# Buffers, order and PSUM sharing in a fused attention and expert kernel: a second fp16 buffer for q and k, later gate transposes, copied logits, earlier gathers

## The chip, the cores and the metric

The kernel runs on one core of one Trainium2 chip. The metric is the device time in microseconds (us) of one execution. A "span" is the time from the first to the last instruction in a profile, 1.4 to 2.1 us shorter than the time of the same execution. Each run has several executions: one with a profile, and, where rounds are named, timed ones that alternate with the kernel before on the same chip.

An execution is marked slow when it is over 1.5% above the fastest of its kernel. On this one core that mark needs care. In five sets of rounds the kernel before spreads from 218.64 us (at a clock of 0.930) to 232.84 us (0.900) without a clear gap. In the first set no execution was below 225 us, and there 9 of the 11 count as fast; in the other sets only one to four do. So I give medians with the lowest and highest, and beside them the ratio of fast runs where there is one.

## The reference

Attention over B=4, H=8, S=768, D=64: three "retrieval" heads (0, 2 and 6) are causal over all keys, the other five see 4 sink keys and a window of 64. Its output, seen as 3072 rows of 512, goes through a mixture of experts that skips some rows:

```python
skip_score = x @ w_skip                      # rows with a score <= 0 stay as they are
logits = x[do_compute] @ w_gate              # 8 experts, the best one is taken
gate_w = softmax(logits)[best]
y[mask_e] = gate_w * (relu(x[mask_e] @ w1[e]) @ w2[e])     # 512 -> 1024 -> 512
out[do_compute] = x + y
```

## The kernel before

Attention works on 16 pairs of heads, four pairs to a batch. The loop tells the work of one iteration; TensorE takes its instructions in exactly this order, the order on the other engines is a scheduler's.

```python
for i in range(NPR + 2):                     # NPR = 16 pairs
    cast_v(i); load_qk(i + 3); load_v(i + 2) # cast: fp32 -> fp16 on GpSimd
    step(0)                                  # a step: score matmuls into PSUM, exp on ScalarE
    transpose(i + 1, "q")                    # TensorE -> tr_psum, copied out by ScalarE
    step(1)
    if i >= 2: gate_transpose(i - 2)         # "xtp": TensorE -> tr_psum, copied out by VectorE
    weigh(i - 1, 0)                          # weighting with v
    step(2)
    transpose(i + 1, "k")                    # TensorE -> tr_psum, "kz" copies, most on VectorE
    cast_qk(i + 2)                           # "qin", "kin" on GpSimd
    step(3)
    weigh(i - 1, 1)                          # ends with the fp16 copy "gx" on GpSimd
    step(4)
    if (i - 2) % 4 == 0 and i > 2: place((i - 2) // 4 - 1)   # counts "kps" in tr_psum
    gate_logits(i - 2)                       # every fourth time: logits "gps" in tr_psum, choose(b)
```

`tr_psum` has two buffers, for the q transposes, the k transposes, the gate transposes, the logits and the counts alike. PSUM is full. The fp32 q, k and v have two buffers each, filled by the sync engine's DMA queue; the expert weights come over GpSimd's queue.

`choose(b)` is a chain of some thirteen small VectorE operations on the logits of a batch (`mx`, `sub`, `eq`, `m2`, `oh`, `rk`, `gate`, `val`). It reads `gpss[b]`, the logits, in PSUM. `place(b)` counts tokens for each expert (matmuls into `kps`) and works out each token's place (`posi`, `Lall`, `Rall` on VectorE). After the last batch the index table `idx_s` is ready, and the expert half starts: gather 128 rows at a time, two matmul groups per expert, scatter.

```python
for e in range(E):
    if e + 1 < E:
        first(e + 1)                         # first matmul group of the next expert
        t = 2 * (e + 4)
        if t < NT: gather(t, t + 2)          # GpSimd: indirect DMA of the rows
        if todo: load_weight()               # GpSimd: 1 MB of weights
    ...
```

The softmax here doesn't subtract the row's maximum and nothing guards it: scores larger than these inputs give would overflow.

## Time and profile before

| | before |
|---|---|
| time, median of the first three runs | 228.5 us (225.91 to 229.19) |
| profiled execution | 221.96 us, span 220.5, clock 0.922 |
| attention, first score matmul to `idx_s` | 11.85 to 134.1 us |
| expert half, `idx_s` to the end | 86.4 us |

The page's first part gives for each engine the busy time, its share of the span and the number of instructions:

```profile
PE 153.5 (70%) x1829; PEld 117.2 (53%) x1829; DVE 127.8 (58%) x307; ACT 95.9 (43%) x134; POOL 131.7 (60%) x206
```

PE is TensorE, DVE VectorE, ACT ScalarE and POOL GpSimd. No engine is full.

### The profile page before, as it was taken

To read this page: it belongs to the slowest core of one execution; us is meant where nothing else is said; L and a number is where in the kernel's file an instruction comes from. 1 tells how busy PE (TensorE), PEld (TensorE's weight loads), DVE (VectorE), ACT (ScalarE), POOL (GpSimd) and SP (SyncE) were. 2 spreads that over 40 slices of the span, in tenths; PEclk is the share of its full clock that TensorE was granted. 3 is DMA by queue.
4 is the path that set the end of the run, shared out by engine and by line. 5 is a ranking of instruction groups with operands and counts; after the bars stand their busy time and mean duration, and the time that the engine had idled before them with its cause. 6 is when DMAs were issued, how large, how long until landed. Compare 5 with 4: busy or idle time off the path is not lost. (4 is left out here: it accounts for less than half of the span.)

```text
span 220.5 us, 4689 instructions
## 1 busy us (share of the span) xinstructions
PE 153.5 (70%) x1829; PEld 117.2 (53%) x1829; DVE 127.8 (58%) x307; ACT 95.9 (43%) x134; POOL 131.7 (60%) x206
## 2 busy tenths in 40 slices
PE   0277777786676569668976620489999999399900
PEld 0256556675465457556865510377866886247300
DVE  7519687669996399966899572342453453121400
ACT  2156875876766584656854210044412431204000
POOL 7999788676873686756765114883678344212510
PEclk9999999999999999988996965589999999969985
DMA  6987999999699997899999978999999999961010
GB/s 158 271 273 191 295 199 328 268 253 307 185 224 253 314 328 183 212 263 197 239 219 245 197 172 174 195 253 251 210 195 214 252 217 265 234 177 56 17 60 1
DMA packets 47982, 47.09 MB, mean 214 GB/s; under 512 B 28484, under 2 KB 43588, under 8 KB 47058
## 3 DMA queue, kind: packets, MB, share of 16 engines
q0 software_dynamic: 7104, 21.56, 46.8%
q1 hardware_dynamic: 40850, 25.17, 41.5%
q8 instruction: 16, 0.26, 0.5%
q14 instruction: 12, 0.10, 0.1%
HBM read 56.64 MB, written 10.49 MB: 304 GB/s over the span
## 5 line engine op out<-in xcount | busy, mean ns | idle before, releaser
L591 ACT ACTIVATE at<-pst 128x1024 f16<-128x1024 f32 (+2 forms) x76 | 61.6, 833 | 41.0 <-PE pst L586 40.8
L918 ACT ACTIVATE ht<-hps 128x512 f16<-128x512 f32 x32 | 19.1, 597 | 54.2 <-PE hps L911 54.2
L586 PE MATMUL pst<-qT,kz 128*128 128x128 f16 (+2 forms) x288 | 36.5, 247 | 0.2
L586 PEld LDWEIGHTS <-kz 128*128 128x128 f16 x288 | 24.4, 103 | 20.6 <-issue 5.6
L930 POOL DMA_INDIRECT out_dram<-xg,idx_s x16 | 16.3, 1019 | 29.0 <-DVE xg L928 21.5
L911 PE MATMUL hps<-xT,w 128*128 128x256 f16 x256 | 30.9, 281 | 1.2 <-DVE xT L901 1.2
L911 PEld LDWEIGHTS <-w 128*128 128x128 f16 x256 | 28.5, 115 | 3.9 <-issue 1.5
L925 PE MATMUL yps<-w,ht 128*128 128x512 f16 x128 | 30.3, 393 | 0.0
L525 DVE COPY kz<-tps 64x768 f16<-64x768 f16 x28 | 26.5, 948 | 6.3 <-PE tps L508 5.9
L928 DVE SCALAR_TENSOR_TENSOR xg<-yps,gsl,xg 128x512 f32<-128x512 f32 x16 | 12.0, 751 | 22.0 <-PE yps L925 22.0
L577 PE MATMUL pst<-smask,ident 128*128 128x512 f16 (+1 forms) x60 | 22.7, 378 | 2.3 <-ACT at L591 2.3
L652 PE MATMUL xtp<-ident,gx 128*128 128x128 f16 x96 | 8.4, 225 | 21.3 <-POOL gx L634 10.4
L875 POOL DMA_INDIRECT xg<-out_dram,idx_s x16 | 16.8, 1052 | 10.1 <-issue 4.0
L489 POOL CAST kin<-kf 128x768 f16<-128x768 f32 x16 | 14.0, 875 | 13.8 <-PE tps L508 13.3
L925 PEld LDWEIGHTS <-ht 128*128 128x128 f16 x128 | 12.7, 101 | 14.6 <-issue 1.9
L611 PE MATMUL opsa<-va,at 128*128 128x65 f16 x372 | 19.9, 196 | 0.0
L652 PEld LDWEIGHTS <-gx 128*128 128x128 f16 x96 | 5.6, 99 | 24.9 <-POOL gx L634 18.1
L626 DVE TENSOR_TENSOR xh<-opsa,rec 128x384 f32<-128x384 f32 x32 | 17.8, 556 | 1.2
L634 POOL CAST gx<-xh 128x768 f16<-128x768 f32 x15 | 12.3, 822 | 10.1 <-DVE xh L626 10.1
L611 PEld LDWEIGHTS <-at 128*128 128x128 f16 x472 | 18.3, 100 | 0.1
L891 DVE CAST x<-xg 128x512 f16<-128x512 f32 x16 | 9.4, 626 | 14.5 <-DMA xg<-out_dram,idx_s 14.5
L495 POOL CAST va<-vf 128x768 f16<-128x768 f32 x16 | 13.2, 828 | 7.1 <-PE opsa L611 5.0
(120 smaller groups left out, 257.7 us busy)
## 6 DMA issues: line engine op xcount, KB each, us to landing
w<-in_moe_w_dram POOLq DMA_DIRECT2D x14, 1024.0 KB, 11.4
qf<-in_q_dram SPq DMA_DIRECT2D x16, 384.0 KB, 5.7
kf<-in_k_dram SPq DMA_DIRECT2D x16, 384.0 KB, 5.0
vf<-in_v_dram SPq DMA_DIRECT2D x32, 192.0 KB, 5.3
out_dram<-xh SPq DMA_DIRECT2D x7, 768.0 KB, 5.3
w<-in_moe_w_dram POOLq DMA_DIRECT2D x4, 512.0 KB, 7.2
out_dram<-xh SPq DMA_DIRECT2D x2, 384.0 KB, 3.7
xg<-out_dram,idx_s POOLq DMA_INDIRECT x16, 6.9
```

The lines of the kernel that those rows point to most:

```text
L489: nc.gpsimd.tensor_copy(h16, qk32[name, i].rearrange("p h n d -> p n h d"))
L525: nc.vector.tensor_copy(to, ti[r])
L577: nc.tensor.matmul(pst[:, bank - c0:bank - c0 + mw], C.ident, neg[:, bank:bank + mw], start=True, stop=False)
L586: nc.tensor.matmul(pst[:, c - c0:c - c0 + n * P], kb, qT[i][:, qb * P:(qb + n) * P], start=mw <= 0, stop=mw <= 0 or (c, j, qb, n) == here[-1])
L591: nc.scalar.activation(ats[i][:, b0:b0 + cn], pst[:, :cn], ACT.Exp, scale=SCALE)
L611: nc.tensor.matmul(opsa[:, qb, :], ats[i][:, b0 + c:b0 + c + P], vb, start=(n == 0), stop=(n == len(plan) - 1))
L626: nc.vector.tensor_mul(xhs[i // 2][:, :, 2 * (i % 2) + hi, :], opsa[:, :, :D], rec.to_broadcast([P, NQB, D]))
L875: ins = nc.gpsimd.indirect_dma_start(out=xgs[t], out_offset=None, in_=out[:, :], in_offset=bass.IndirectOffsetOnAxis(ap=idx_s[:, t:t + 1], ...
L911: nc.tensor.matmul(hps[:, fi, :], wts[e, 0][:, s].rearrange("p (t c r) -> p t r c", c=P, r=WR)[:, fs // WR, fs % WR], xTs[e][:, s, :], sta ...
L918: nc.scalar.activation(ht[:, 2 * f2:2 * f2 + 2], hps, ACT.Relu)
L925: nc.tensor.matmul(yps, hts[e][:, fs, s2 * P:(s2 + 1) * P], wts[e, 1][:, fs, :], start=(fs == 0), stop=(fs == FS - 1))
L930: ins = nc.gpsimd.indirect_dma_start(out=out[:, :], out_offset=bass.IndirectOffsetOnAxis(ap=idx_s[:, t:t + 1], axis=0), in_=xgs[t], in_off ...
```

## The change

The intent is to take away waits in front of the gate transposes (by asking for them later, and by freeing the PSUM buffer of the logits at once), a wait of GpSimd (by second fp16 buffers), and a hole before the last expert (by gathering its rows earlier).

```diff
-         tc.tile_pool(name="qk_in", bufs=1) as qk_in_pool, \
+         tc.tile_pool(name="qk_in", bufs=2) as qk_in_pool, \
@@ choose(b)
-            lg, skip = gpss[b][:, :, :E], gpss[b][:, :, E]
+            glog = gpss[b]
+            if b < B - 1:
+                glog = small("glog", [P, NQB, E + 1])
+                nc.vector.tensor_copy(glog, gpss[b])
+            lg, skip = glog[:, :, :E], glog[:, :, E]
@@ the attention loop
                 step(1)
-                if i >= 2:
-                    gate_transpose(i - 2)
                 ...
                 step(3)
+                if i >= 2:
+                    gate_transpose(i - 2)
@@ the expert loop
-                    t = 2 * (e + 4)
-                        gather(t, t + 2)
+                    t = 4 * (e + 2)
+                        gather(t, t + 4)
```

## The prediction

> **What bounds the kernel now.** The program has two halves: attention (16 head pairs, four to a batch, gating of the finished batch woven in), and the expert part (gather, two matmuls per expert, scatter). No engine is full over the span (TensorE 70%, VectorE 58%, GpSimd 60%), so I first cut the span into stages at the places where the timeline shows the first score matmul of each group of four pairs, and asked for busy time in those stretches. Columns: stretch, its length, busy time and count on TensorE, weight loads, VectorE, ScalarE, GpSimd, then clock, DMA share, GB/s.
>
> ```profile
> 11.85:37.24 25.39, 19.65 (x265) 15.50 (x265) 16.35 (x27) 18.03 (x24) 22.25 (x36) 1.00 0.95 252
> 37.24:63.72 26.48, 20.52 (x339) 16.54 (x339) 22.33 (x57) 18.80 (x26) 19.92 (x32) 1.00 0.96 261
> 63.72:93.08 29.36, 20.52 (x339) 16.55 (x339) 23.49 (x58) 18.80 (x26) 19.18 (x31) 1.00 0.96 249
> 93.08:122.90 29.82, 22.82 (x327) 18.31 (x327) 23.61 (x59) 18.32 (x25) 18.20 (x31) 0.89 1.06 232
> ...
> 141.90:189.00 47.10, 46.32 (x352) 35.41 (x351) 18.88 (x34) 16.15 (x28) 28.21 (x31) 0.96 1.04 234
> 189.00:198.20 9.20, 5.58 (x24) 2.54 (x25) 2.70 (x5) 0.57 (x1) 0.66 (x2) 0.81 0.83 205
> ```
>
> In attention the fullest engine is VectorE, but only at 22.33/26.48 = 84%, 80% and 79% in groups 2 to 4 (64% in the first, which has no gating). So attention is bound by waits round a loop of engines, with VectorE closest behind. In the expert part TensorE is full (46.32 of 47.10 us) until 189, and then has a hole.
>
> Next, the waits of the attention stages: who waited for whom, total, times, longest.
>
> ```profile
> PE xtp L652 <- POOL gx L634: 10.4, 7, 2.3
> PE pst L577 <- ACT at L591: 5.8, 10, 0.8
> PE xtp L652 <- DVE rk L719: 4.8, 3, 1.8
> PE xtp L652 <- DVE posi L756: 4.6, 3, 1.9
> ```
> ```profile
> DVE gxT L660 <- PE xtp L652: 13.9, 8, 3.3
> ```
> ```profile
> POOL kin L489 <- PE tps L508: 13.3, 10, 2.3
> ```
>
> TensorE loses 10.4 + 4.8 + 4.6 = 19.8 us in front of one operation, the gate transpose (xtp): 10.4 because GpSimd has not yet cast the attention output to fp16 (gx), 9.4 because the shared PSUM buffer it wants is still held by the routing logits (read last by rk) or by the routing counts. VectorE then idles 13.9 us in front of the copy of that transpose, and GpSimd 13.3 us because its one fp16 k buffer is still being transposed. The chain that ended last holds only two pieces at the very end (0.5% of the span) and does not help here.
>
> The hole at 189 is in the timeline:
>
> ```profile
> 188.97 0.60 ACT L918 ACTIVATE ht<-hps 128x512 f16<-128x512 f32 x1 [0.28 <-PE hps L911]
> 191.83 1.13 DVE L891 CAST x<-xg 128x512 f16<-128x512 f32 x2 [5.60 <-DMA xg<-out_dram,idx_s]
> 192.49 0.23 PEld L898 LDWEIGHTS <-x 128*128 128x128 f16 x4 [3.83 <-DVE x L891]
> 192.50 1.13 PE L898 MATMUL xtp<-ident,x 128*128 128x128 f16 x8 [3.56 <-DVE x L891]
> ```
>
> The last expert's rows are gathered too late: GpSimd issued the second of those gathers at 179.7, after 2.6 us of its own waiting for an earlier weight load, and its rows landed some 11 us later.
>
> **What the Trainium skill says.** "Perfetto Trace Analysis", section Optimization Strategy, says that a gap repeating on the engine that should be saturated can mean too few buffers for the next tile. The trace agrees: the gap in front of xtp repeats in 13 of the iterations, 0.5 to 2.3 us each. "TensorE: Matmul & The Clock Gate", Part 1, says that the clock drops to half after about 3.4 us of idleness and needs about as long of work to come back. The trace fits: after the 3.56 us hole the clock of that stretch is 0.81, and the 16 matmuls that begin at 193.42 run 4.95 us until the next group starts, where the 16 that begin at 181.82 run 3.46. "SBUF — State Buffer", section Who interferes with whom, says that VectorE in a two-port mode and GpSimd block each other for whole instructions. The trace fits that too: one form of copy, 64x20 (kx), takes 146 ns at least and 2447 ns at most. So a VectorE packed more tightly beside GpSimd will not reach 100%.
>
> **The change, part by part.**
>
> *Gate transpose later.* On TensorE's list it moves from before the first weighting to after the k transposes, that is behind 0.3 to 0.7 us of weighting, 0.3 of k transposes and about 1.2 of scores: 1.8 to 2.2 us by the timeline around 46 to 48.7. The waits for gx are 0.5 to 2.3 us, so practically all of the 10.4 us goes. The two PSUM buffers are then taken in the order q, k, gate transpose, not q, gate transpose, k. That puts the next waiter on the logits' or counts' buffer at the k transposes, later in the iteration.
>
> *Logits copied out.* One added VectorE copy in each of three batches, about 0.2 us each by the reduction that reads the same logits (202 ns): +0.6 us of VectorE. It frees the PSUM buffer before the choice of experts, which takes about 4 us from mx to the last val. With the new order the 4.8 us go; the 4.6 us for the counts go mostly through the order alone.
>
> *Two buffers for fp16 q and k.* Removes GpSimd's 13.3 us of waiting, which helps only because the late casts stand in front of gx on the same engine and hold the load buffers. No instruction is added.
>
> *Sum for attention.* 19.8 us of TensorE waits are removed, but I don't count them all: behind them stands VectorE. Group by group I let VectorE run at 92%, my choice, between the 84% of now and the full use that the blocking by GpSimd forbids; its busiest 10 us stretches show 95%. Group 2: (22.33 + 0.2)/0.92 = 24.5 for 26.48, gain 2.0. Group 3: 23.7/0.92 = 25.8 for 29.36, gain 3.6. Group 4: 23.8/0.92 = 25.9 for 29.82, gain 3.9. Group 1 isn't VectorE bound: the one wait there, 2 us, goes. Together 11.5. Another 1 us from the tail, where the first weighting of the last pair no longer stands behind the gate transpose; and 2 us back, because weight loads and q, k, v loads are squeezed into less time (v issues already stall on their queue, up to 9.5 us at 93). Attention: minus 10.5 us.
>
> *Gathers four at a time.* Eight gathers are issued in the first two turns and not in four. An issue costs GpSimd about 1.3 us (1.04 plus 0.3), so in turns 0 and 1 the weight loads start 2.7 us later each, and in turns 2 and 3 earlier; the last weight load goes out some 7 us sooner. The last gathers are issued near 164, not 180, and needed near 188. The first matmuls of successive experts start at 155.49, 162.88, 170.28, 177.67, 185.06 and 198.16: 7.39 us apart, but 13.10 the last time. The excess, 5.7 us (3.6 wait, 1.5 slow clock, 0.6 transposes that no longer overlap), should go. I count 4.5, since the DMA engines are at 1.04 in this stage and a late weight may take the place of the late rows.
>
> Sum: 10.5 + 4.5 = 15 us of 220.5, leaving 205.5, or 6.8%.
>
> **Rivals.**
> (a) VectorE takes over at once: its gating work is lumped (the choice in one iteration of four, the counts in the next), so TensorE waits there instead, for kz or for PSUM. For it: 95% in the stretches with gating, at 50 to 60, 80 to 90 and 110 to 120. Against: two weighting buffers and two score buffers give some slack. Then attention gains only 5 us, in all 9 to 10, and the profiled span is 211.
> (b) DMA takes over. For it: share 0.95 to 1.06 throughout and stalls of the queue that loads v. Against: it moved 323 GB/s at 70 to 80 us but 215 at 80 to 90, so it has room. If attention is cut and the expert part then starves for weights, the gain of one half is lost: 212 to 214.
> (c) VectorE packs almost fully and the hole goes wholly: 11.5 + 4 + 5.7, some 21 us, 199 to 200.
> (d) The early gathers delay weights of experts 4 and 5. Against: those have 10 us and more between landing and use. It would cost at most the 4.5 us.
>
> **Range and chances.** The profiled execution (222 us in all) is quicker than the timed ones (225.9 to 229.2), so I scale: 228.5 x 205.5/220.5 = 213. As the timed executions may have a lower clock, with less to gain from waits, I say 214. The range 208 to 221 spans rival (c) to rivals (a) and (b): 228.5 x 200/220.5 = 207 and 228.5 x 213/220.5 = 221. Over 2% faster means below 223.9: only if two rivals meet. Chances 0.91 faster, 0.07 within, 0.02 slower.
>
> **What would show it.** Right: no wait of TensorE for gx over 1 us in total; the group of waits for rk and posi below 2 us; GpSimd's wait for the k transposes gone; groups 2 to 4 at 24 to 26 us with VectorE at 90% or more; successive experts 7.4 us apart to the end with no wait for a gather after 150. Wrong: a new wait of similar size at the k transposes or the weighting; VectorE still near 80% in groups 2 to 4; expert matmuls that wait for weights; the first gather, now 5 us from issue to landing, queued behind weights.

## The result, and the profile after

| | before | after |
|---|---|---|
| median | 228.45 us, 4 runs (225.91 to 229.19) | 220.86 us, 4 runs (219.36 to 222.55) |
| ratio of fast runs | | 0.9689, interval 0.9599 to 0.9779 |
| span of the profile | 220.5 us | 218.4 us |
| `idx_s` ready | 134.1 us | 137.4 us |
| from `idx_s` to the end | 86.4 us | 81.0 us |

A ratio is the mean time of one kernel's fast runs over that of the other's in the same rounds, so not quite the ratio of the medians quoted. The change is 3.1% faster. The expert half gained 5.4 us, for 4.5 foretold. The attention half of these two profiles lost 3.3 us, where 10.5 should have come.

The same stretches as in the prediction, cut at the first score matmul of each group of four pairs, then the tail up to `idx_s`, then the stretch in which the hole was. Columns: stretch, its length, busy time and count on TensorE, weight loads, VectorE, ScalarE, GpSimd, then clock, DMA share, GB/s.

```profile
11.92:36.24 24.32, 19.66 (x264) 15.61 (x264) 16.44 (x26) 17.87 (x23) 21.40 (x35) 1.00 0.88 225
36.24:66.77 30.53, 23.47 (x342) 19.34 (x340) 23.60 (x58) 18.64 (x26) 21.47 (x33) 0.89 0.91 262
66.77:92.11 25.34, 20.43 (x340) 16.88 (x339) 23.53 (x56) 18.47 (x26) 20.41 (x32) 1.00 1.03 281
92.11:125.68 33.57, 23.16 (x326) 18.66 (x326) 24.08 (x63) 18.00 (x24) 16.02 (x28) 0.85 0.89 200
125.68:137.40 11.72, 6.05 (x103) 5.32 (x101) 8.32 (x34) 1.22 (x3) 1.82 (x4) 0.65 0.89 175
...
189.00:198.00 9.00, 9.00 (x71) 6.94 (x70) 4.10 (x7) 2.77 (x5) 2.83 (x4) 1.00 1.03 217
```

Of groups 2 to 4 only the third did what was expected: 25.34 us with VectorE at 23.53/25.34 = 93%. The second group became 4 us longer than before (30.53 for 26.48), the fourth, 33.57 us, is the longest of all, and both have a clock of 0.85 to 0.89. TensorE is full from 189 to 198: the hole is gone.

The waits of the same profile (who waited for whom: total, times, longest):

```profile
POOL va L495 <- DMA vf<-in_v_dram: 9.7, 1, 9.7
PE kps L747 <- DVE kz L525: 8.2, 3, 3.5
PE xtp L652 <- POOL gx L634: 8.1, 4, 4.7
...
POOL kin L489 <- DMA kf<-in_k_dram: 4.1, 5, 1.7
...
POOL qin L489 <- DMA qf<-in_q_dram: 3.6, 1, 3.6
```

The waits of the gate transposes for `rk` and `posi` are gone, and GpSimd's 13.3 us of waiting for the k transposes too (which part of the change removed that is asked below). In their place stand three new things. The counts (`kps`) wait 8.2 us for VectorE's copies of k. GpSimd waits 9.7 us, once, for a v load, and 7.7 us for q and k loads. The gate transposes still wait 8.1 us for GpSimd's copy `gx`.

The single wait of 9.7 us in GpSimd's own timeline (start, length, engine, line, operation, and in brackets the idle time before it):

```profile
110.90 0.85 POOL L501 COPY vx<-va 4x325 f16<-4x325 f16 x2
121.42 0.83 POOL L495 CAST va<-vf 128x768 f16<-128x768 f32 x1 [9.67 <-DMA vf<-in_v_dram]
```

And the same cast, of the same pair 15, in the profile before:

```profile
114.43 0.82 POOL L495 CAST va<-vf 128x768 f16<-128x768 f32 x1 [1.70 <-PE opsa L611]
```

The second half of pair 15's v was asked for at 103.19 us and landed at 121.27, 18.1 us later; before it was asked for at 104.44 and landed 4.7 us later. I counted the DMA records of the two queues by microsecond in the trace of the changed kernel:

```
us      GpSimd's queue (weights)             sync engine's queue (v, results)
106      0 records                           461 records
108     27, median 0.32 us each              489, median 0.02 us each
110     50, median 0.32                       21, median 0.03
112     51, median 0.32                       24, median 0.03
116     23, median 0.62                       10, median 0.03
119      5                                   373, median 0.05
```

As long as large weight records run, the v load gets only one small record for every two of them. The Trainium skill, "DMA: Bandwidth & Descriptors", section Queues, rings and completion order, says that a DMA engine takes turns between the queues it has work for, packet by packet. The traces agree in part. In the second profile of the kernel before (b_again, below) the counts are about equal, 53 and 50 records in the microsecond from 112, 29 and 30 in that from 114, with 0.3 to 0.6 us a record on one side and 0.03 on the other. In the changed kernel they are two to one; no run here shows why.

### The profile page after: what moved, and what is told of

The parts are those of the page before. A ratio compares the mean times of both kernels' runs of the same rounds, so it can differ in the third digit from the quotient of the medians.

```text
span 218.4 us, 4660 instructions
## 1 busy us (share of the span) xinstructions
PE 156.9 (72%) x1829; PEld 122.1 (56%) x1829; DVE 129.4 (59%) x310; ACT 95.4 (44%) x134; POOL 132.4 (61%) x206
## 5 line engine op out<-in xcount | busy, mean ns | idle before, releaser
L591 ACT ACTIVATE at<-pst 128x1024 f16<-128x1024 f32 (+2 forms) x76 | 60.7, 836 | 44.7 <-PE pst L586 44.5
L586 PE MATMUL pst<-qT,kz 128*128 128x128 f16 (+2 forms) x288 | 38.5, 255 | 2.0 <-DVE kz L525 1.9
L586 PEld LDWEIGHTS <-kz 128*128 128x128 f16 x288 | 25.4, 106 | 25.5 <-issue 9.2
L915 PE MATMUL hps<-xT,w 128*128 128x256 f16 x256 | 31.5, 285 | 1.2 <-DVE xT L905 1.2
L934 POOL DMA_INDIRECT out_dram<-xg,idx_s x16 | 16.8, 1052 | 22.6 <-DVE xg L932 19.1
L929 PE MATMUL yps<-w,ht 128*128 128x512 f16 x128 | 28.8, 379 | 0.0
L611 PE MATMUL opsa<-va,at 128*128 128x65 f16 x372 | 21.7, 203 | 0.0
L495 POOL CAST va<-vf 128x768 f16<-128x768 f32 x16 | 13.3, 832 | 13.3 <-DMA vf<-in_v_dram 9.7
L611 PEld LDWEIGHTS <-at 128*128 128x128 f16 x472 | 20.2, 105 | 1.0 <-issue 0.5
L489 POOL CAST qin<-qf 128x768 f16<-128x768 f32 x16 | 14.3, 891 | 9.8 <-DMA qf<-in_q_dram 3.6
L929 PEld LDWEIGHTS <-ht 128*128 128x128 f16 x128 | 12.3, 98 | 13.4
L905 DVE COPY xT<-xtp 128x512 f16<-128x512 f16 x16 | 6.1, 420 | 14.8 <-PE xtp L902 14.7
L516 ACT ACTIVATE qT<-tps 128x768 f16<-128x768 f16 x16 | 12.9, 805 | 4.5 <-PE tps L508 4.5
```

Source lines behind the costliest of these rows:

```text
L489: nc.gpsimd.tensor_copy(h16, qk32[name, i].rearrange("p h n d -> p n h d"))
L586: nc.tensor.matmul(pst[:, c - c0:c - c0 + n * P], kb, qT[i][:, qb * P:(qb + n) * P], start=mw <= 0, stop=mw <= 0 or (c, j, qb, n) == here[-1])
L591: nc.scalar.activation(ats[i][:, b0:b0 + cn], pst[:, :cn], ACT.Exp, scale=SCALE)
L611: nc.tensor.matmul(opsa[:, qb, :], ats[i][:, b0 + c:b0 + c + P], vb, start=(n == 0), stop=(n == len(plan) - 1))
L915: nc.tensor.matmul(hps[:, fi, :], wts[e, 0][:, s].rearrange("p (t c r) -> p t r c", c=P, r=WR)[:, fs // WR, fs % WR], xTs[e][:, s, :], sta ...
L929: nc.tensor.matmul(yps, hts[e][:, fs, s2 * P:(s2 + 1) * P], wts[e, 1][:, fs, :], start=(fs == 0), stop=(fs == FS - 1))
```

## The experiments

All 18 runs gave correct results. The five sets of rounds ran on chips 0, 6, 15, 0 and 12, and each has its own runs of the kernel before: 227.31 us (225.25 to 228.99) in the first, 225.71 (221.06 to 227.81) in the second, 227.08 (221.33 to 230.6) in the third, 227.4 (223.75 to 229.19) in the fourth, 226.85 (218.64 to 232.84) in the fifth, 11 runs each.

| run | what | median us (lowest to highest) | ratio of fast runs | `idx_s` in its profile |
|---|---|---|---|---|
| first set | | | | |
| b_again | before, unchanged | 227.48 (226.49 to 228.29) | 1.0033 | 139.0 |
| g_only | gathers only | 223.02 (214.85 to 224.85) | none | 139.8 |
| attn_only | the attention parts only | 224.15 (222.82 to 226.13) | 0.9906 | 136.6 |
| a_again | the change, unchanged | 220.42 (217.49 to 221.59) | 0.9636 | 137.9 |
| second set | | | | |
| w_move | change, weight loads moved | 222.93 (221.74 to 224.64) | 1.0014 | 141.3 |
| v3 | change, third v buffer | 213.60 (210.66 to 215.78) | 0.9504 | 130.4 |
| p_early | change, counts earlier | 223.04 (220.5 to 224.87) | 0.9958 | 139.4 |
| tl_only | later transposes and logits copy | 221.23 (220.2 to 225.74) | 0.9936 | 132.1 |
| third set | | | | |
| tlg | change without second q, k buffers | 215.49 (214.65 to 216.56) | 0.9701 | 132.2 |
| v3_tlg | tlg with third v buffer | 213.03 (212.12 to 214.72) | 0.9600 | 131.5 |
| v3_again | v3 once more | 213.62 (210.15 to 216.48) | 0.9522 | 127.1 |
| b_v3 | before with third v buffer | 219.81 (216.2 to 220.65) | 0.9773 | 131.2 |
| fourth set | | | | |
| ch | change, choice later | 218.80 (215.91 to 224.7) | 0.9615 | 134.8 |
| v3_ch | v3, choice later | 217.70 (216.34 to 221.68) | 0.9630 | 135.8 |
| v3_tlg_ch | v3_tlg, choice later | 214.94 (214.45 to 216.15) | 0.9541 | 131.7 |
| v3_few | v3, four weight loads out of attention | 234.90 (233.29 to 236.53) | 1.0414 | 129.3 |
| fifth set | | | | |
| v3_kz | v3_tlg, four copies to ScalarE | 213.08 (212.76 to 214.24) | none | 130.9 |
| v3_kzx | v3_kz, 15 more copies to ScalarE | 206.69 (205.14 to 208.11) | none | 123.0 |

In the second and third set the fast runs of before are only its two or three quickest (221.06, 222.35 and 224.34; 221.33 and 222.78), so those ratios make the gains look smaller than the medians do. Neither is wrong; they answer to different parts of the spread. With so few fast runs the verdicts at 2% are weak: a_again is faster, b_again and attn_only are the same, g_only, v3_kz and v3_kzx have none, and all others are unclear. So I also read the stages in the profiles. A difference between runs of two sets is one between chips too.

### Was the first profile of the kernel before a typical one, and what is each half worth?

**b_again** and **a_again** have no edit. **g_only** has only the last part of the diff (gathers), **attn_only** all the others.

> The kernel before, unchanged, run and profiled once more. Its first profile (221.96 us) was 4 to 7 us quicker than its timed executions (225.91 to 229.19). Theory 'lucky profile': the first profile is not the typical execution; this one comes out at 226 to 229 and shows more waiting in the attention half (longer waits in front of the gate transpose, or for a v load), with the idea that some load sometimes lands late. Rival 'clock': the waits are the same within 1 us and the granted clock is lower, below 0.90. Ratio to itself 1.00 within 0.5%.

> Before, with only the gathers four at a time. By the two traces the hole of 5.7 us in front of the last expert should go: theory 'the gain is the gathers' expects 4.5 to 6 us less, ratio 0.974 to 0.980, first matmuls of successive experts 7.4 us apart to the end. Rival 'the weights are next': the late rows are replaced by late weights of the last expert and the ratio is above 0.99.

> The changed kernel without the new gathers: two buffers, later gate transpose, copied logits. Theory 'the gain is the gathers': the three attention parts together are worth nothing, ratio 0.99 to 1.01, with the waits of TensorE for gx cut but 5 to 10 us of new waits (routing counts behind the k copies, GpSimd casts that wait for loads). Rival 'attention does gain in the typical execution': ratio 0.975 to 0.985, because the first profile of before was a quick one.

> The changed kernel, unchanged, profiled once more. In its first profile one v load of 192 KB took 18.1 us to land (the others 2.8 to 11.7) and held GpSimd for 9.7 us and TensorE for 4.7. Theory 'built in': the same load of the last pair is late again, by 14 us or more, since weight packets of 0.3 to 0.6 us alternate with its packets of 0.02. Rival 'chance': it lands in under 8 us this time and the span is 3 to 5 us shorter than 218.4. Ratio to before 0.96 to 0.98.

The waits of the second profile of the unchanged kernel before:

```profile
PE xtp L652 <- POOL gx L634: 17.9, 8, 7.1
...
POOL va L495 <- DMA vf<-in_v_dram: 8.2, 1, 8.2
```

The late v load is in the kernel before as well. The first profile, on which the prediction rests, was an execution without it: 221.96 us against 227.48. The clock is not what differs by much (0.922 and 0.911). In this profile, of an execution of 228.29 us, the gate transposes wait not 10.4 but 17.9 us for `gx`; the copy stands behind the cast of v on GpSimd.

The gathers alone bring 227.31 - 223.02 = 4.3 us, and on top of the attention parts 224.15 - 220.42 = 3.7. Predicted were 4.5. One of the six executions of g_only took 214.85 us; it has no profile, so why is open. Beside it the other five are marked slow, so there is no ratio; but the profiles agree. From `idx_s` to the end it is 85.8 to 87.7 us in the five with the old gathers (before, b_again, attn_only, tl_only, b_v3), and 80.0 to 81.4 in seven with the new ones (g_only, after, a_again, tlg, v3, v3_again, v3_tlg), so some 5 to 6 us. The attention parts alone bring 227.31 - 224.15 = 3.2 us (2.4 by the means of the fast runs), not 10.5. So the failed term is in attention.

### Is it the late v load?

**v3** gives v a third buffer and asks for it three pairs ahead; **b_v3** does the same to the kernel before; **w_move** leaves the buffers and moves the weight loads away from the late pairs.

```diff
 v3, b_v3
-            vf = ld_pool.tile([P, 2, NQB, D], FP32, tag="vf", name="vf")
+            vf = ld_pool.tile([P, 2, NQB, D], FP32, tag="vf", name="vf", bufs=3)
             load_qk(2)
+            load_v(2)
-                if i + 2 < NPR:
-                    load_v(i + 2)
+                if i + 3 < NPR:
+                    load_v(i + 3)
 w_move
-                if i in (0, 5, 10, 11, 12, 13):
+                if i in (0, 3, 5, 7, 9, 13):
```

> The changed kernel, but the weight loads that hung on the fp16 attention outputs of pairs 0, 5, 10, 11, 12 and 13 now hang on pairs 0, 3, 5, 7, 9 and 13, so that no weight packets run beside the late v loads. Theory 'starved load' (the second half of pair 15's v is held up for 17 to 19 us because weight packets of 0.3 to 0.6 us take turns with its packets of 0.03 us, GpSimd waits some 10 us for it, and the copies for the gate behind it wait too): the wait of the cast of v for its load falls from 10.8 us to under 3, the wait of the gate transposes for GpSimd's copy from 10.9 to under 6, and the time to 0.97 to 0.985 of the changed kernel (214 to 217 us). Rival 'VectorE or PSUM bound anyway': the load wait goes but another wait of the same length takes its place, time within 1% of 220.4. Rival 'the load is late for another reason' (issue order on the sync engine's queue): the wait stays at 8 to 11 us.

> The changed kernel with a third buffer for the fp32 v, and v loaded three pairs ahead instead of two; the weights stay where they were. 'Starved load': pair 15's v is asked for about 6 us earlier, so it has that much less of the weights in its way or has 6 us more to land; the wait of the cast of v falls from 10.8 us to 0 to 5, and the time to 215 to 218. 'VectorE or PSUM bound anyway': within 1% of 220.4.

> The kernel before with the third v buffer alone. 'The late v is in both kernels and not of the change': its wait for the v load of pair 15 (8.2 us) goes, its time falls to 219 to 222, idx_s from 139 to 133 to 134, and it no longer jumps by 4 us and more between executions. Rival 'only the changed kernel has room to gain from it': 225 to 227. If the attention parts are worth what the prediction said once v is in time, this stays 6 us or more behind v3 in the time when idx_s is ready; if they are worth little, 3 us or less.

> The changed kernel with the third v buffer once more, for comparison in the same rounds: 212 to 215 us, no wait of the cast of v for its load, idx_s ready at 130 to 132.

With the third buffer the wait of the cast of v for its load is gone from the profiles of all kernels that have it. It is worth 227.08 - 219.81 = 7.3 us to the kernel before, and 220.42 - 213.6 = 6.8 us to the changed one (of different sets). By the means of the fast runs alone it is 5.0 (222.1 and 217.0) and 6.9 (218.9 and 212.0). The spread of b_v3 is still 4.45 us, where I expected it to go, so the late load is not its only cause. So the late load was not made by the change and is not what the change lost. Its cause is confirmed by where it went in w_move, a miss of my expectation:

```profile
POOL qin L489 <- DMA qf<-in_q_dram: 11.5, 3, 5.5
...
PE xtp L652 <- POOL gx L634: 13.5, 6, 3.9
```

Pair 15's v then landed in 4.9 us, but the weights, moved to earlier pairs, held up q loads there (11.5 us), and the time was 222.93. Moving the large loads moved the wait; a buffer more removed it.

With v in time, before and change differ by 219.81 - 213.62 = 6.2 us in one set of rounds (5.6 by fast runs). From `idx_s` to the end it is 86.6 us in the profile of b_v3 and 81.0 and 81.3 in those of v3 and v3_again, so all but about 1 us of this is the gathers. The waits of the gate transposes in the profile of b_v3 (an execution of 219.81 us, one of its four that are marked slow, at clock 0.928):

```profile
PE xtp L652 <- POOL gx L634: 9.5, 8, 2.1
...
PE xtp L652 <- DVE posi L756: 4.6, 3, 1.9
PE xtp L652 <- DVE rk L719: 4.4, 3, 1.8
```

That is 18.5 us, about the 19.8 us of the first profile. In v3 the first is 2.6 us and the other two are absent, yet `idx_s` comes at 130.4 and 127.1 us instead of 131.2. Some 16 us of waiting removed, 1 to 4 us gained. This is the real question.

### The second buffers for fp16 q and k

**tl_only** is the kernel before with the later gate transposes and the copied logits only. **tlg** is the change without the second buffers, **v3_tlg** the same with the third v buffer:

```diff
-         tc.tile_pool(name="qk_in", bufs=2) as qk_in_pool, \
+         tc.tile_pool(name="qk_in", bufs=1) as qk_in_pool, \
```

> The kernel before with the gate transposes half a pair later and the logits copied out, without the second fp16 q and k buffers and with the old gathers. All three attention parts together gave 224.2 us against 227.3. If the second buffers lose by pulling the casts ahead of their loads and so delaying the copies for the gate, this is as fast or faster than that: 221 to 224, with no waits of the q cast for its load. If the buffers are what gained (no wait of GpSimd for the k transposes), this is 225 to 227.5 and that wait of 12.6 us is back. The wait of the counts for the k transposes' copies (9.7 us with all three) should be here too, as it comes of the order of the PSUM buffers: over 4 us.

> The changed kernel with one buffer instead of two for fp16 q and k (the other three parts stay). The later gate transposes with copied logits and the old gathers ran 221.2 us, with the second buffers 224.2. Theory 'the second buffers hurt': their casts are pulled ahead of their loads on GpSimd and the v loads start 5 us later, so without them and with the new gathers (4.4 us) this is 216 to 218 us, idx_s is ready by 132 to 133 us instead of 137 to 138, and the gate transposes wait under 4 us for GpSimd's copies. Rival 'chance': the difference was which rounds had the late v, and this is 220 to 221 like the changed kernel, idx_s at 137.

> As the last one (one buffer for fp16 q and k) with the third buffer for the fp32 v and v loaded three pairs ahead. 'The second buffers hurt only through the late v': with v in time they no longer hurt and their own gain (GpSimd does not wait for the k transposes) is left, so this is 1 to 3 us slower than v3: 214 to 217. 'The second buffers hurt in themselves': 1 to 3 us faster than v3: 210 to 213.

Without them the change is faster: 215.49 us, against 220.42 with them (in another set, with nearly the same time of before). Against the medians of before the gain is 227.08 - 215.49 = 11.6 us with the second buffers left out and 227.31 - 220.42 = 6.9 with them. They cost 4.7 us (3.5 by the means of the fast runs alone, 218.9 and 215.4). With the old gathers they cost 1.3 by these gains (4.5 and 3.2), 3.4 by the means of the fast runs (224.3 and 220.9). The ratios to before don't show it (0.9636 with and 0.9701 without, 0.9906 and 0.9936), for the reason given below the table, but the stage does: `idx_s` is ready at 136.6 to 137.9 us in three profiles with second buffers and at 132.1 and 132.2 in the two without. In tlg the late half of v is asked for at 98.91 us instead of 103.19 and still takes 18.4 us to land, so it comes 3.9 us earlier, at 117.34; and the gate transposes wait 3.9 us for `gx`, not 8.1 to 10.9. With v in time no harm is seen, and no sure good: 213.03 without and 213.62 with by the medians, 213.2 and 211.4 by the means of the fast runs. The expectation of 214 to 217 or 210 to 213 was met by neither side clearly.

GpSimd's wait of 12.6 us for the k transposes should have been back in tl_only, which has one buffer. It was not: its cast `kin` no longer waits for them there, and of the waits for `tps` only this one is left, nearly all of it a single wait:

```profile
POOL qin L489 <- PE tps L508: 5.8, 3, 5.0
```

So the later gate transposes with the copied logits removed that wait, and not the second buffers, to which the prediction gave it. What it was worth by itself no run tells. Why the scheduler asks for v later with the second buffers I did not test.

### Did the wait for a PSUM buffer go, or only move?

In v3_tlg no load is late and the gate transposes no longer wait. What is left in its profile:

```profile
PE kps L747 <- DVE kz L525: 12.8, 3, 4.6
```

The timeline of the changed kernel shows how this wait arises (VectorE's lines of the first gating, left out in part):

```profile
53.50 0.65 DVE L723 TENSOR_SCALAR rk<-glog 128x6 f32<-128x6 f32 x1
...
55.10 1.33 DVE L718 TENSOR_TENSOR oh<-eq,m 128x48 f16<-128x48 f32 x1
...
58.33 1.91 DVE L525 COPY kz<-tps 64x768 f16<-64x768 f16 x2
...
60.30 0.20 PE L747 MATMUL kps<-acc,ones 128*128 128x48 f16 x1 [3.48 <-DVE kz L525]
...
61.93 1.02 ACT L591 ACTIVATE at<-pst 128x1024 f16<-128x1024 f32 x1 [5.03 <-PE pst L586]
```

VectorE does the choice of experts from 53.14 to 57.94, then the weighting's output, and only at 58.33 the copies of k. The counts need the PSUM buffer of these k transposes. TensorE stands for 3.48 us, and ScalarE 5.03 us for the next scores. Two ways round it:

**p_early** tells the counts before the k transposes; **ch**, **v3_ch** and **v3_tlg_ch** tell the choice half a pair later, behind the copies of k, and the counts a pair later.

```diff
 p_early
                 step(1)
+                if (i - 2) % 4 == 0 and i > 2:
+                    place((i - 2) // 4 - 1)
                 ...
-                    if (i - 2) % 4 == 0 and i > 2:
-                        place((i - 2) // 4 - 1)
 ch
-                choose(b)                              # in gate_logits
+                glogs[b] = small("glog", [P, NQB, E + 1])
+                nc.vector.tensor_copy(glogs[b], gpss[b])
                 ...
                     weigh(i - 1, 1)
+                if (i - 2) % 4 == 0 and i > 2:
+                    choose((i - 2) // 4 - 1)
-                    if (i - 2) % 4 == 0 and i > 2:
-                        place((i - 2) // 4 - 1)
+                    if (i - 3) % 4 == 0 and i > 3:
+                        place((i - 3) // 4 - 1)
```

> The changed kernel with the matmuls that count the tokens of each expert moved from after the gate transposes of their iteration to before them and before the k transposes, so that the shared PSUM buffer is asked for in the order q, counts, k, gate transposes. Theory 'new wait': the counts no longer wait for VectorE's copies of the k transposes (6.1 to 9.7 us in three places before), the time falls by 2 to 4 us to 216 to 218. Rival 'VectorE bound there': the same VectorE work is only waited for elsewhere (k transposes or weighting), time within 1% of 220.4.

> The changed kernel with VectorE's choice of experts (thirteen small operations, 4 to 6 us together) told half a pair later: the logits are copied out at once, the choice follows after the next k transposes and the counts a pair later still, for all batches but the last. Theory 'VectorE lump' (the waits for the PSUM buffer did not go, they moved from the gate transpose, 9 us, to the counts, 6 to 10 us, since the counts' buffer is that of the k transposes, which VectorE copies only after the choice): the wait of the counts for the copies of k falls under 3 us and the time by 2 to 4 us, to 216.5 to 218.5. Rival 'VectorE has no room': it waits elsewhere for the same time (scores for kz, weighting), time within 1% of 220.5.

> The same on top of the third v buffer (213.6 us): 'VectorE lump': 209.5 to 212, idx_s at 125 to 128 us instead of 127 to 130; 'no room': 213 to 215.

> The same on top of the third v buffer with one buffer for fp16 q and k (213.0 us): 'VectorE lump': 209 to 211.5; 'no room': 212.5 to 214.5.

Both take the wait away that they aim at, and both get another. In p_early the counts wait 6.3 us for `oh`, a late step of the choice, and the time is 223.04, against 220.4 of the changed kernel in another set. In ch:

```profile
PE pst L586 <- DVE kz L525: 9.2, 5, 3.0
```

The scores now wait for the copies of k. In v3_ch it is 12.7 us and in v3_tlg_ch 11.8. The times are 217.7 and 214.94, slower than without (213.6 and 213.03) and slower than either theory said. ch itself is 218.8 against 220.4; three of its executions are at 216 to 218 and three at 220 to 225. The fast ones alone have a mean of 217.0 against 218.9, which would fit "VectorE lump", so ch stays open. With v in time the rival "no room" is the nearer one: wherever the wait is put, TensorE waits for VectorE about as long (10.0 us became 12.7, 12.8 became 11.8).

### DMA or VectorE?

**v3_few** takes four of the six weight loads out of attention. It must be slower as a whole, and only `idx_s` is asked for.

```diff
-                if i in (0, 5, 10, 11, 12, 13):
+                if i in (0, 5):
```

> The kernel with the third v buffer, with four of the six weight loads taken out of the attention half (those of pairs 10 to 13) and left to the expert half, which must then wait for weights: the whole time will be worse, 222 to 232. What is asked is only the time when idx_s is ready. Theory 'the last groups of attention are held up by the weight stream on the DMA engines': idx_s at 123 to 126 us, 3 us or more earlier than 127 to 130. Rival 'with v in time DMA no longer bounds attention': 127 to 130.5 as before.

It is 234.9 us, even slower than the 222 to 232 expected, and `idx_s` is ready at 129.3 us, between the 130.4 and 127.1 of the two profiles of v3. With v in time the weight stream does not bound attention, though the DMA share of these stretches is 0.90 to 1.05.

**v3_kz** and **v3_kzx** take work off VectorE and give it to ScalarE.

```diff
 v3_kz: the second k copy of the last pair of each batch (4 copies of 0.95 us)
-                if hi == 0 or IS_RETR[heads(i)[1][0]]:
+                if hi == 0 or (IS_RETR[heads(i)[1][0]] and i % 4 != 3):
                     nc.vector.tensor_copy(to, ti[r])
                 else:
                     nc.scalar.activation(to, ti[r], ACT.Copy)
 v3_kzx: that, and the copies of the gate transposes (15 of 0.56 us)
-                nc.vector.tensor_copy(xTg, xtp)
+                nc.scalar.activation(xTg, xtp, ACT.Copy)
```

> One buffer for fp16 q and k, third v buffer (213.0 us, the steadiest of the fast ones), with one copy of k in four pairs moved from VectorE to ScalarE: the second half of the k transposes of the last pair of each batch, 0.95 us, three of which lie just behind the choice of experts, while ScalarE sits idle. Theory 'VectorE bounds attention where the gating is' (the wait moved, but was the same size, when the choice was told later): the wait of the counts for the copies of k falls from 12.8 to 9 to 11 us, idx_s comes 1.5 to 3 us earlier than 131.5 and the time is 210.5 to 212. Rival 'TensorE's slow clock or the order of its own list bounds': 212.5 to 213.5, no change.

> As the last one, with the copies of the gate transposes (15 of 0.56 us) moved from VectorE to ScalarE too, some 12 us less for VectorE and as much more for ScalarE. 'VectorE bounds': 207 to 211, idx_s at 126 to 129. 'ScalarE is as near its bound': the exponentials come later, TensorE's wait for a score buffer grows from 9 to 13 us and more, time 212 to 216.

v3_kz missed: 213.08 us, no gain, as its rival had it (212.5 to 213.5). The wait of the counts did fall, from 12.8 to 7.5 us, and is now put down to the copy of the gate transposes; VectorE's busy time did not fall (135.9 us for 135.0). v3_kzx gained a little more than expected (207 to 211): 206.69 us, 6.4 us less than v3_kz in the same rounds and 6.3 less than v3_tlg, with `idx_s` at 123.0 instead of 130.9 and 131.5. Its wait of the counts and its groups 2 to 4, and those groups of v3_tlg below:

```profile
PE kps L747 <- ACT gxT L660: 2.6, 3, 0.9
```
```profile
36.14:60.58 24.44, 20.26 (x339) 16.96 (x339) 20.27 (x47) 21.98 (x31) 19.29 (x32) 1.00 1.05 298
60.58:86.64 26.06, 20.70 (x339) 16.93 (x339) 24.41 (x57) 21.99 (x31) 19.76 (x31) 1.00 1.08 286
86.64:111.45 24.81, 19.84 (x326) 16.15 (x326) 23.14 (x52) 20.96 (x29) 17.14 (x29) 1.00 1.07 239
```
```profile
36.16:65.50 29.34, 22.71 (x339) 18.85 (x339) 26.31 (x59) 18.59 (x26) 19.91 (x32) 0.88 0.90 256
65.50:93.60 28.10, 21.98 (x340) 18.28 (x339) 25.07 (x58) 18.59 (x26) 19.31 (x31) 0.88 0.97 255
93.60:120.51 26.91, 20.84 (x326) 17.16 (x326) 24.47 (x58) 17.53 (x24) 17.21 (x29) 0.94 1.05 241
```

In v3_tlg VectorE is 89 to 91% busy in these groups (26.31/29.34, 25.07/28.10, 24.47/26.91), and the clock is 0.88 to 0.94. With the copies gone from VectorE the waits are short, the clock stays at 1.00, and TensorE does the same 339 matmuls of group 2 in 20.26 us instead of 22.71. So what stood in VectorE's queue bounded these groups. A high busy share alone does not say so: in v3_kzx VectorE is 83 to 94% busy in groups that are shorter. Whether by the sum of its work or by the place of these copies behind the choice is not separated: v3_kzx changes both, and v3_kz, which took 3.8 us off, gained nothing.

v3_kzx is the fastest kernel. Against 226.85 us of before in its rounds it takes 20.2 us off, 8.9% by the medians (only one of the 11 executions of before counted as fast there, so there is no ratio).

## Why the prediction was right or wrong

**What held.** The gathers: predicted 4.5 us, measured 4.3 alone and 3.7 on top by the medians, 5 to 6 by the spans after `idx_s`. The hole is gone. The gate transposes' waits for `rk` and `posi` are gone. So is GpSimd's wait for the k transposes, but not by the second buffers (tl_only). The first group and the tail gained what was said: with v in time 25.39 to 23.50 us and 13.09 to 10.96 (b_v3 and v3_tlg), predicted 2 and 1. Rival (d) did not come. A first sign of rival (b) is there: the last expert's first matmuls waited for their weights:

```profile
196.46 3.42 PEld L915 LDWEIGHTS <-w 128*128 128x128 f16 x32 [0.36 <-DMA w<-in_moe_w_dram]
```

The wait is 0.36 us, so it costs nothing yet.

**The base.** The prediction scaled the profile of 221.96 us to 228.5 and laid the difference to the clock, "as the timed executions may have a lower clock". The runs showed a late load in its place: the v load of pair 15 took 16.8 us in b_again where it took 4.7 in the first profile. The prediction saw v stalls "up to 9.5 us at 93" and did not ask what a later stall would hit. Giving v a third buffer is worth 5 to 7 us in either kernel, and the change has no part in that.

**"Practically all of the 10.4 us goes".** Moving the gate transposes by 2 us was measured against waits of at most 2.3 us. In the second profile of the kernel before the waits for `gx` reach 7.1 us, since `gx` stands behind the cast of v. In the changed kernel 8.1 and 10.9 us remained. With v in time the step is right: 9.5 us in b_v3, 2.6 in v3.

**"The 4.8 us go; the 4.6 us for the counts go mostly through the order alone".** This is the step that failed by its mechanism. The prediction itself noted that the next waiter on the shared buffer comes "at the k transposes, later in the iteration", and counted that as harmless. In fact the counts come to stand behind the copies of k, which VectorE makes only after the choice: 9.0 us of waits for `posi` and `rk` (b_v3) became 8.4 to 12.8 us for `kz` (v3_again, v3, v3_tlg). The prediction's list of wrong signs has it, "a new wait of similar size at the k transposes or the weighting", and rival (a) tells it: VectorE's gating work is lumped, TensorE waits there for kz or for PSUM, attention gains only 5 us, profiled span 211. With v in time and without the second buffers the span was 211.5, but that number is met by chance: against b_v3 (217.8) the gain is all in the expert half, and `idx_s` is at 131.5 us instead of 131.2.

**"Logits copied out ... +0.6 us of VectorE".** The copies cost that, 3 of 0.20 us. But the operations that read the logits changed too. The groups of instructions by line show it, first before, then after (count, busy time in us, mean ns):

```profile
L719 DVE TENSOR_SCALAR rk<-gps 128x6 f32<-128x6 f32 x4 | 0.6, 158 | 0.0
```
```profile
L723 DVE TENSOR_SCALAR rk<-glog 128x6 f32<-128x6 f32 x3 | 1.9, 650 | 0.0
```

The same operation on six elements per partition takes 158 ns from PSUM and 650 ns in the mean from the copy in SBUF. The Trainium skill, "SBUF — State Buffer", section Who interferes with whom, says that VectorE meets GpSimd where it has two SBUF inputs or works in a two-port mode, and names this kind of operation among those that can. The traces agree: in the changed kernel GpSimd casts beside each of the three, and the first of them ends at 54.15 us, with the cast that began at 53.29 and took 0.83. In v3 one of the three, beside a memset on GpSimd, took 0.17 us from the same copy in SBUF. The prediction cited this rule for VectorE's ceiling, and did not apply it to the operations whose input it saw moved to SBUF. Three times 0.5 us is a small part of what follows, though.

**"Group 2: (22.33 + 0.2)/0.92 = 24.5".** The 92% was nearly right, 89 to 91% in v3_tlg. The busy time was wrong: 26.31 us in group 2, not 22.53, then 25.07 for 23.7 and 24.47 for 23.8. An instruction that is held up counts as busy, as `rk` shows, and busy time grew: over the whole span VectorE is busy 125.5 to 127.8 us in the four profiles of kernels with the old attention (before, b_again, g_only, b_v3), and 129.4 to 135.0 in the eight that have the later transposes and no further edit to VectorE's work or order (after, a_again, attn_only, tl_only, tlg, v3_tlg, v3, v3_again). Only 0.6 us of that are new instructions. With v in time the largest growth of one kind is in the 64x320 copies of k, whose operands did not move: between 12 and 140 us they take 7.5 us in b_v3, 9.7 to 12.3 in v3, v3_again and v3_tlg; the cause of that was not tested. So the groups took 29.34, 28.10 and 26.91 us. Those of b_v3, with the old attention:

```profile
37.27:63.34 26.07, 20.52 (x339) 16.54 (x339) 21.94 (x57) 18.69 (x26) 19.94 (x32) 1.00 1.00 270
63.34:92.53 29.19, 22.11 (x339) 17.87 (x339) 23.90 (x58) 18.80 (x26) 19.18 (x31) 0.94 0.96 250
92.53:118.15 25.62, 19.37 (x327) 15.81 (x326) 21.19 (x55) 17.33 (x24) 18.02 (x30) 1.00 1.06 234
```

That is 80.9 us in all before, and 84.4 in v3_tlg (80.6 in v3_again), where the prediction had 76.2: with the late v out of the way, its 9.5 us for these groups are missing altogether. That the groups can run at 24.4 to 26.1 us, which the prediction had for them, v3_kzx shows, but with 12 us taken off VectorE.

**"Two buffers for fp16 q and k".** Predicted to remove GpSimd's 13.3 us and so to help where late casts hold up `gx`. That wait goes without them too (tl_only). With them GpSimd ran into late q and k loads (7.7 us), and v came later. They cost 1.3 to 4.7 us with the late v; without it no cost and no sure gain is seen.

**The sum.** Predicted 10.5 + 4.5 us of 220.5. Measured some 4 to 6 us for the gathers and 3.2 for attention. Of the attention term, the parts without the second buffers gave 4.5 us by the medians (tl_only against before, same rounds; the ratio of fast runs, 0.9936 with an interval of 0.9817 to 1.0055, leaves room for nothing at all), and the buffers took part of it back. The later transposes and the copied logits were never run apart.

## What to carry to other kernels

Before you subtract a wait, ask which buffer or engine the next instruction in the same order will want, and what stands in front of it there: here the wait for the shared PSUM buffer stayed with the engine that empties it, whatever the order of those who ask. Profile the kernel before twice when its profiled time lies outside its timed ones; here one quick execution hid 5 to 7 us that hung on a single late load. And count an engine's busy time as a thing that a change can lengthen: here by up to 9 us, with 0.6 us of new instructions.

## What the Trainium skill lacked or had wrong

- "DMA: Bandwidth & Descriptors", Queues, rings and completion order, has the taking of turns by packets; the traces agree in part (53 records to 50, but also 51 to 24). It lacks what that means for a load of small pieces on another queue: with weight records of 0.32 to 0.62 us beside it, a v load took 16 to 19 us, in the kernel before and after alike, where the v loads of each profile have a median of 5.0 to 5.8.
- "Perfetto Trace Analysis", Optimization Strategy, says that a gap repeating on the engine that should be saturated can mean too few buffers. Neither case here fits that: GpSimd's gap that repeated ten times (12.6 us, for the k transposes) went by the order of the work and the copied logits, with no buffer more for `kin` (tl_only), while a gap that came once (8.2 us, the late v) was worth 5 to 7 us for one buffer more.
- "SBUF — State Buffer", Who interferes with whom, has the rule; the runs add a size for the case that an operand is moved out of PSUM: 158 to 650 ns for six elements per partition beside a cast on GpSimd.
- "TensorE: Matmul & The Clock Gate", Part 1, has the clock drop to half after an idle window of about 3.4 us. The runs fit in part: with waits of the counts of up to 4.6 us the clock of groups 2 and 3 was 0.88 (v3_tlg), with none over 0.9 us it was 1.00 (v3_kzx); but it was 0.94 in v3_again too, where no single wait of TensorE in these groups was over 3.0 us. Beside the slower clock the same 339 matmuls of group 2 took 2.45 us more, half of the 4.90 by which that group was longer.
- No page that I read says how far executions of one program on one core spread: here from 218.64 to 232.84 us, with clocks from 0.930 to 0.896.
